# Output projection in 15 products a block: the last two heads' rows moved into spare rows by small DMAs

## The chip, the core and the metric

The kernel runs on one core of a Trainium2 chip. TensorE (PE in the profile, PEld for its weight loads), VectorE (DVE), ScalarE (ACT) and GpSimd (POOL) each work through their own list of instructions in order; SyncE (SP) does nothing but issue transfers. A transfer is issued by an instruction on SP's or ACT's list and carried out by 16 DMA engines. The metric is the time of one execution on the device, in microseconds (us), as the median of several runs.

## The reference

x has 2048 tokens of 640 features. Both branches read the normalised x; the result is x plus their product.

```python
def _A_ref(x, wqkv, w_phi, wo):                  # 32 heads of 20
    q, k, v = ...                                # x @ wqkv, per head
    pq = jnp.einsum("bhsd,hdf->bhsf", q, w_phi)
    pk = jnp.einsum("bhsd,hdf->bhsf", k, w_phi)
    phi_q = jnp.concatenate([_softmax(pq), _softmax(-pq)], axis=-1)   # 40 a head
    phi_k = jnp.concatenate([_softmax(pk), _softmax(-pk)], axis=-1)
    kv = jnp.einsum("bhsf,bhsd->bhfd", phi_k, v)
    z = jnp.einsum("bhsf->bhf", phi_k)
    num = jnp.einsum("bhqf,bhfd->bhqd", phi_q, kv)
    den = jnp.einsum("bhqf,bhf->bhq", phi_q, z)[..., None] + 1e-6
    return heads_joined(num / den) @ wo

xn = _layernorm(x)
s = _A_ref(xn, A_wqkv, A_w_phi, A_wo)
g = _silu(gelu(xn @ w1 + b1) @ w2 + b2)
return x + s * g
```

## The kernel before

The work is laid out by hand in the order in which PE runs it. First come keys, values and queries (up to about 238 us of the profile), with the state kv summed in PSUM and the exponentials of the queries stored in e_dram. Then follow twelve units of the MLP (`for unit in range(units)`, 238 to 555 us): in each, `part` makes the up products and `down` the down products (L998), whose sums VectorE adds to y (L1007). Beside the units the queries are normalised, one tile of 128 tokens after another: `q_load` (L1041), `q_norm` with a multiplication on GpSimd, sums on VectorE, a scaling on GpSimd, a transpose in blocks on VectorE (L1064), and four stores (L1069) into phi_t, which holds the query features with the tokens along the free axis. phi_t has one DRAM tensor for each of the four chunks of 512 tokens; chunk c holds tiles 4c to 4c+3. Tile 7, the last one, is done only after the units, by the generator `late_q`, one step of which runs after each block of the output projection (two steps after each of the first two).

The last stage, from 555 us on, is the subject. It takes the chunks in the order 2, 3, 0, 1 (ORDER). The loop at L1343 runs over the chunks, and within it over five blocks d of 128 output columns; blocks are numbered here 0 to 19 in the order of time.

- `load_phi` (L1091, L1093) loads a chunk's query features, 1280 rows: five tiles phT of 240 rows, three heads to each 60 rows of output, and a sixth with the last 80 rows (heads 30 and 31).
- `num` makes the state products: two for each of the five tiles (L1103, weights bdk), which give 64 rows of output each, of which 60 are heads and 4 are zeros; and two for the sixth (L1110, weights bdl), in which the two heads' 40 rows stand three times. ACT copies a PSUM bank rounded to fp32r (L1106, L1112), VectorE subtracts the copy from the bank (L1107, L1113), so that oT holds a high and a low part.
- `finish` is one block: 16 products (L1156), three for each of the five tiles (high by high, high by low, low by high) and one for the last 40 rows, whose three forms stand side by side in 120 rows. Its weight wol is made once by `make_wol` on VectorE (L1080, L1081). VectorE multiplies the sum by the gate (L1158), GpSimd adds x (L1159), SP stores (L1163). The last block runs in two halves of 256 columns.
- `first_num` makes the first chunk's state products within the last down products (`down` asks it for a step ahead of each of its five sums). For the others, `num` stands after the fourth block (d == 3) of the chunk before.
- `load_res` loads x (L1130) and, for the first two chunks, the gate (L1134), four blocks ahead; `gate` computes it on ACT for the other two (L1142).

All engines keep the written order here (`manual_schedule`). PSUM has eight banks (`bankB`), handed on as soon as what reads them is done.

Of the kernel before, what the change touches and what calls it, by code (L numbers as in the profile page):

```python
# [8 lines left out]
F32 = mybir.dt.float32  # L9
# [6 lines left out]
P = 128  # L16
# [30 lines left out]
def hedgehog_gated_mlp_kernel(ctx: ExitStack, tc: tile.TileContext, x, xt_in, wqk, bd, wv, wo, w1, b1, w2, b2, out_t):  # L47
# [72 lines left out]
    for h in range(3):  # L120
# [4 lines left out]
    lowsel = const.tile([P, 1], F32, name="lowsel")  # L125
    nc.gpsimd.memset(lowsel[:], -1.0)
    nc.gpsimd.affine_select(out=lowsel[:], in_=lowsel[:], pattern=[[0, 1]],
                            compare_op=OP.is_ge, fill=0.0, base=-80, channel_multiplier=1)
    midsel = const.tile([P, 1], F32, name="midsel")
    nc.gpsimd.memset(midsel[:], -1.0)  # L130
    nc.gpsimd.affine_select(out=midsel[:], in_=midsel[:], pattern=[[0, 1]],
                            compare_op=OP.is_ge, fill=0.0, base=-40, channel_multiplier=1)
    nc.gpsimd.affine_select(out=midsel[:], in_=midsel[:], pattern=[[0, 1]],
                            compare_op=OP.is_ge, fill=0.0, base=79, channel_multiplier=-1)
    const.tile([P, 8], F32, name="align")
    bdk = const.tile([P, 10, 64], F32, name="bdk")
    bdl = const.tile([P, 120], F32, name="bdl")
# [781 lines left out]
    def kv_state(kvr):  # L919
        nc.gpsimd.memset(bdk[:, :, 60:], 0.0)  # L920
        ps = bankB()
# [14 lines left out]
        for r in range(3):  # L936
            nc.vector.tensor_tensor(bdl[:80, 40 * r:40 * r + 40].rearrange("p (h d) -> p h d", d=20),
                                    ps[:80, None, 352:372].to_broadcast([80, 2, 20]),
                                    mask[:80, :2, None].to_broadcast([80, 2, 20]), op=OP.mult)
# [131 lines left out]
    def wol_raw():  # L1071
        raw = row([P, D], F32, "raw")
        for r in range(3):
            nc.sync.dma_start(raw[40 * r:40 * r + 40, :], wo[640:680, :])
        return raw

    def make_wol(raw):
        wol_h = row([P, D], F32R, "wolh")
        wol = row([P, D], F32R, "wol")
        nc.vector.tensor_copy(wol_h[:120, :], raw[:120, :])  # L1080
        nc.vector.scalar_tensor_tensor(wol[:120, :], wol_h[:120, :].bitcast(F32), midsel[:120, :], raw[:120, :],  # L1081
                                       op0=OP.mult, op1=OP.add)
        return wol


    def load_phi(c, js, home=None):
        out = {}
        for j in js:
            ph = slab(F32, "phT", (P, 2, CW)) if home is None else home.tile([P, 2, CW], F32, tag="L", name="phT")
            if j < 5:  # L1090
                nc.sync.dma_start(ph[:120], phi_t[c][240 * j:240 * j + 240, :].rearrange("(e p) t -> p e t", p=120))  # L1091
            else:
                nc.sync.dma_start(ph[:80, 0], phi_t[c][1200:, :])  # L1093
            out[j] = ph
        return out

    def num(phi, oT, js):
        for j in js:
            ph = phi.pop(j)
            po = bankB()  # L1100
            if j < 5:
                for e in range(2):
                    nc.tensor.matmul(po[64 * e:64 * e + 64, :], bdk[:120, 2 * j + e, :], ph[:120, e, :],  # L1103
                                     start=True, stop=True)
                o2 = oT[0][j]
                nc.scalar.activation(o2[:, 0], po[:], AF.Copy)  # L1106
                nc.vector.tensor_tensor(o2[:, 1], po[:], o2[:, 0].bitcast(F32), op=OP.subtract)  # L1107
            else:
                for a, b in ((0, 64), (64, 120)):
                    nc.tensor.matmul(po[a:b, :], bdl[:80, a:b], ph[:80, 0], start=True, stop=True)  # L1110
# [301 lines left out]
```

## Time and profile before

| | us |
|---|---|
| median of 3 runs (650.46 to 650.9) | 650.58 |
| span of the profiled execution | 649.0 |
| PE busy in it | 643.7 (99%) |
| last stage: start of the output projection to PE's end | 555.35 to 645.12 |
| output projection, all L1156 products, share of the chain that ended last | 11% |
| state products, L1103, share of the chain | 2% |
| transfers issued by SP, share of the 16 DMA engines, 520 to 650 us | 85.0% |

The profile has one row for an instruction or a group: start, busy time, engine, line, operation, output and inputs, and in brackets what ended the idle time before it. The chain of waits goes back from the last instruction, at each step to what released it. A product of full-precision fp32 (L1103, L1110) stands in it as two records. Rows of SPq and ACTq are issues of transfers; their duration is that of the issue, and the time to landing is a column of its own in the DMA and tile views.

### The profile page before, as it was taken

The page shows a single profiled execution, that of the slowest core. Times are in us where ns is not written, and L with a number is a line of the kernel's source. Part 1 is how long each engine was busy: PE and PEld are TensorE (multiplying, and loading weights), DVE is VectorE, ACT ScalarE, POOL GpSimd, SP SyncE. Part 2 cuts the span into 40 slices and gives each one's busy share as a digit, 9 for nine tenths or more (in the row PEclk, how much of TensorE's full clock was granted, in tenths as well). Part 3 has the DMA queues.
Part 4 walks back from the last instruction along what each step waited for, and adds up shares of the span by engine and source line. Part 5 has one row for each costly group of instructions (what it writes and reads, how often), then busy time and mean ns, then how long its engine had stood idle before and what let it go on. Part 6 is the DMA issues. An engine that isn't in the chain of part 4 may idle for free.

```text
span 649.0 us, 11412 instructions
## 1 busy us (share of the span) xinstructions
PE 643.7 (99%) x4379; PEld 559.1 (86%) x4379; DVE 485.1 (75%) x736; ACT 238.1 (37%) x345; POOL 408.9 (63%) x375
## 2 busy tenths in 40 slices
PE   9999999999999999999999999999999999999997
PEld 9999999999999998888888888888888886766866
DVE  5887976789867787587988877768889899853132
ACT  3622423425243447244243346641231524032130
POOL 2876477897987756857878865355463966342321
PEclk9999999999999999999999999999999999999999
DMA  9477286494312477365986998794969499999952
GB/s 346 113 238 228 57 303 197 107 309 147 123 42 74 152 263 262 103 217 170 317 236 236 254 409 285 144 350 163 183 238 243 67 267 198 304 242 248 291 207 81
DMA packets 167119, 136.53 MB, mean 210 GB/s; under 512 B 89890, under 2 KB 131106, under 8 KB 166682
## 3 DMA queue, kind: packets, MB, share of 16 engines
q1 hardware_dynamic: 164330, 124.22, 65.9%
q10 hardware_dynamic: 2736, 11.60, 4.8%
q8 instruction: 34, 0.56, 0.4%
q14 instruction: 19, 0.16, 0.1%
HBM read 87.41 MB, written 48.38 MB: 209 GB/s over the span
## 4 chain that ended last, share of the span: by engine, by line
PE 96%; DMA 1%; DVE 1%; SPq 0%; issue 0%; DVEq 0%
PE pB L998 24%; PE pA L411 23%; PE pB L969 23%; PE pB L1156 11%; PE pA L724 6%; PE pB L1103 2%; PE pA L174 2%; PE kv L491 2%; PE qV L724 1%; DMA folds<-in_wqk_dram 1%; PE qY L724 1%; DVE y L1007 1%; PE pB L1110 1%; DMA phi_t<-eq 0%; PE pA L397 0%; DVE wolh L1080 0%
## 5 line engine op out<-in xcount | busy, mean ns | idle before, releaser
L998 PE MATMUL pB<-hs,w2s 128*128 128x512 f32 x720 | 165.7, 389 | 0.0
L998 PEld LDWEIGHTS pB<-hs,w2s 128*128 128x128 f32 x720 | 135.0, 188 | 28.8 <-DVE y L1007 0.8
L969 PE MATMUL pB<-xp,w1s 128*128 128x512 f32 x324 | 81.3, 389 | 0.0
L969 PE MATMUL pB<-xd,w1s 128*128 128x512 f32 x324 | 79.3, 389 | 0.0
L452 POOL TENSOR_TENSOR eq<-eq,rc 128x1280 f32<-128x1280 f32 x16 | 37.9, 2368 | 55.3 <-DVE rc L1060 38.1
L1156 PE MATMUL pB<-oT,wo 128*128 128x512 f32 (+1 forms) x315 | 72.3, 381 | 0.0
L969 PEld LDWEIGHTS pB<-xd,w1s 128*128 128x128 f32 x324 | 60.8, 188 | 12.6
L969 PEld LDWEIGHTS pB<-xp,w1s 128*128 128x128 f32 x324 | 60.8, 188 | 12.6
L1156 PEld LDWEIGHTS pB<-oT,wo 128*128 128x128 f32 x315 | 57.2, 188 | 13.8 <-PE pB L1103 2.5
L1007 DVE TENSOR_TENSOR y<-pB,y 128x512 f32<-128x512 f32 x100 | 63.1, 676 | 1.4 <-PE pB L998 1.4
L974 ACT ACTIVATE pB<-pB,b1t 128x512 f32<-128x512 f32 x48 | 31.8, 662 | 78.8 <-DVE pB L1237 28.9
L411 PE MATMUL pA<-wk,xp 128*128 128x320 f32 x384 | 59.6, 310 | 0.0
L439 ACT ACTIVATE e<-e 128x1280 f32<-128x1280 f32 x32 | 40.6, 1272 | 50.0 <-POOL e L430 50.0
L411 PEld LDWEIGHTS pA<-wk,xp 128*128 128x128 f32 x384 | 56.9, 188 | 0.1
L430 POOL TENSOR_TENSOR e<-nr,e 128x640 f32<-128x640 f32 x32 | 46.0, 1437 | 16.4 <-DVE nr L429 16.3
L452 POOL TENSOR_TENSOR e<-e,rc 128x1280 f32<-128x1280 f32 x16 | 37.8, 2369 | 20.2 <-DVE rc L479 20.2
L1047 POOL TENSOR_TENSOR ez<-eq,zrep 128x1280 f32<-128x1280 f32 x16 | 47.3, 2959 | 2.0 <-DMA eq<-e_dram 2.0
L519 POOL TENSOR_TENSOR w1s<-raw,w1s 128x640 fp32r<-128x640 f32 (+1 forms) x18 | 26.2, 1458 | 27.6 <-ACT w1s L518 27.6
L411 PE MATMUL pA<-wv,xp 128*128 128x320 f32 x240 | 37.0, 310 | 0.0
L1159 POOL TENSOR_TENSOR xres<-gt,xres 128x256 f32<-128x256 f32 x20 | 14.3, 735 | 35.3 <-DVE gt L1158 24.9
L149 POOL TENSOR_TENSOR w2s<-raw,w2s 128x640 fp32r<-128x640 f32 x23 | 36.1, 1592 | 0.2 <-ACT w2s L147 0.2
L411 PEld LDWEIGHTS pA<-wv,xp 128*128 128x128 f32 x240 | 35.5, 188 | 0.1
(190 smaller groups left out, 1140.4 us busy)
## 6 DMA issues: line engine op xcount, KB each, us to landing
raw<-in_w_dram SPq DMA_DIRECT2D x42, 320.0 KB, 6.7
e_dram<-e ACTq DMA_DIRECT2D x16, 640.0 KB, 3.9
eq<-e_dram SPq DMA_DIRECT2D x16, 640.0 KB
phi_t<-eq SPq DMA_DIRECT2D x64, 160.0 KB, 4.3
phT<-phi_t SPq DMA_DIRECT2D x20, 480.0 KB, 10.1
xt<-in_x_dram SPq DMA_DIRECT2D x16, 320.0 KB, 6.1
xres<-in_xt_dram SPq DMA_DIRECT2D x20, 256.0 KB, 9.1
out_dram<-xres SPq DMA_DIRECT2D x18, 256.0 KB, 5.1
```

The costliest lines, as they stand in the source:

```text
L149: eng.tensor_tensor(sl[:, 1, :], raw, sl[:, 0, :].bitcast(F32), op=OP.subtract)
L411: nc.tensor.matmul(ps[:, hf, :HALF], stat_x(q, o, k, a), ws[k][:, b, hf * HALF:(hf + 1) * HALF], start=n == 0, stop=n == 3 * KC - 1)
L430: rest = lambda: nc.gpsimd.tensor_tensor(e5[:, :, :, 1, :], nr[:, :, :, None].to_broadcast([P, 2, 16, DH]), e5[:, :, :, 0, :], op=OP.subtract)
L439: nc.scalar.activation(ef, ef, AF.Exp)
L452: nc.gpsimd.tensor_tensor(e3, e3, rc[:, :, None].to_broadcast([P, 64, DH]), op=OP.mult)
L724: nc.tensor.matmul(bank[ch], q_x(blk, a, q), p_weight(base, f, w, k)[:, b], start=ch not in seen and n == 0, stop=n == len(mms) - 1, skip_ ...
L969: nc.tensor.matmul(bank[ch][:], tl[:, a, off + wo_:off + wo_ + P], mov(blk, b), start=new and n == 0, stop=n == len(mms) - 1, skip_group_c ...
L974: nc.scalar.activation(ps, ps, AF.Gelu_apprx_tanh, bias=b1t[:, f:f + 1])
L998: nc.tensor.matmul(ps[:], ws[i][:, b, d * P:(d + 1) * P], hs[o][i][:, a, :], start=i == n == 0, stop=(i, n) == (GF - 1, 2), skip_group_che ...
L1007: nc.vector.tensor_tensor(y, ps[:], y, op=OP.add)
L1047: nc.gpsimd.tensor_tensor(zv, ef, zf, op=OP.mult)
L1156: nc.tensor.matmul(ps[:, mv], w, o[:, mv], start=n == 0, stop=n == 15, skip_group_check=True)
```

## The change

The two heads that had a 16th product of their own are put into the rows that stood at zero: each of the ten 64-row groups has four spare rows, and 10 x 4 = 40. The weight wo gets rows 600 to 639 in these places (in the host's layout), and a block has 15 products. The 40 rows of the output come from `num_rest`: one pair of state products for two chunks at once, the first chunk's in rows 0 to 63 and the second's in rows 64 to 127 of one bank, split into high and low part oR as before. `put_rest` then moves four rows of oR into each half of each oT tile by a DMA on ACT's queue, ten a chunk of 4 rows x 4 KB, each once the tile's own split is written.

The order changes with it. `load_rest` loads the last 80 rows for two chunks: for chunks 2 and 3 on SP's queue in the last unit, for chunks 0 and 1 on ACT's queue after block 5. The pair of `num_rest` for chunks 0 and 1 stands on PE after block 7, before that chunk's other state products. `num` stands after the third block of the chunk before (d == 2, not 3), and in `first_num` one step earlier. `late_q` takes two steps after each of the first three blocks, not only after the first two, so the stores of tile 7 come after block 3 and not after block 4. wol, its loads, and the masks lowsel and midsel are gone.

```diff
 def kv_state(kvr):
     nc.gpsimd.memset(bdk[:, :, 60:], 0.0)
+    nc.gpsimd.memset(bdl[:, 40:], 0.0)
...
-        for r in range(3):
-            nc.vector.tensor_tensor(bdl[:80, 40 * r:40 * r + 40].rearrange("p (h d) -> p h d", d=20),
+        nc.vector.tensor_tensor(bdl[:80, :40].rearrange("p (h d) -> p h d", d=20),
...
+    def load_rest(cs, eng):
+        ph = slab(F32, "phR", (P, 2, CW))
+        for c in cs:
+            eng.dma_start(ph[:80, c % 2], phi_t[c][1200:, :])
+        return ph
+
+    def num_rest(ph):
+        po = bankB()
+        for e in range(2):
+            nc.tensor.matmul(po[64 * e:64 * e + 64, :], bdl[:80, :], ph[:80, e, :], start=True, stop=True)
+        o2 = slab(F32R, "oR", (P, 2, CW))
+        split_o(po, o2)
+        return o2
+
+    def split_o(po, o2):
+        nc.scalar.activation(o2[:, 0], po[:], AF.Copy)
+        nc.vector.tensor_tensor(o2[:, 1], po[:], o2[:, 0].bitcast(F32), op=OP.subtract)
+
+    def num(c, phi, oT, oR):
+        for j in range(KC):
+            ph = phi.pop(j)
+            po = bankB()
+            for e in range(2):
+                nc.tensor.matmul(po[64 * e:64 * e + 64, :], bdk[:120, 2 * j + e, :], ph[:120, e, :],
+                                 start=True, stop=True)
+            split_o(po, oT[j])
+            if j:
+                put_rest(c, j - 1, oT, oR)
+        put_rest(c, KC - 1, oT, oR)
+
+    def put_rest(c, j, oT, oR):
+        for e in range(2):
+            r = 64 * (c % 2) + 4 * (2 * j + e)
+            nc.scalar.dma_start(oT[j][64 * e + 60:64 * e + 64].bitcast(F32), oR[r:r + 4].bitcast(F32))
...
-        steps = [(wo_s[j][:, b, d * P:(d + 1) * P], oT[0][j][:, a, :]) for j in range(5) for a, b in PASSES]
-        steps.append((wols[0][:120, d * P:(d + 1) * P], oT[1][:120, 1, :]))
+        steps = [(wo_s[j][:, b, d * P:(d + 1) * P], oT[j][:, a, :]) for j in range(KC) for a, b in PASSES]
...
-            phi = load_phi(ORDER[0], range(6))
+            phi = load_phi(ORDER[0], range(KC))
+            phr = load_rest(ORDER[:2], nc.sync)
...
-        if not more:
-            wolr = wol_raw()
...
     def first_num():
-        wols.append(make_wol(wolr))
-        yield
-        yield
-        yield
-        num(phi, oT, range(6))
+        oR.append(num_rest(phr))
+        yield
+        yield
+        num(ORDER[0], phi, oT, oR[-1])
         yield
...
-            if ci == 0 and d < 2:
+            if ci == 0 and d < 3:
                 next(lq, None)
...
-            if ci + 1 < NCH and d == 3:
-                num(phin, oTn, range(6))
-            if ci + 2 < NCH and d == 3:
+            if ci == 1 and d == 0:
+                phr = load_rest(ORDER[2:], nc.scalar)
+            if ci + 1 < NCH and d == 2:
+                if ci == 1:
+                    oR.append(num_rest(phr))
+                num(ORDER[ci + 1], phin, oTn, oR[-1])
+            if ci + 2 < NCH and d == 2:
                 phin = {**phi, **load_phi(ORDER[ci + 2], JB)}
...
-    wo = np.zeros((680, D), a["wo"].dtype)
+    wo = np.zeros((D, D), a["wo"].dtype)
     for k in range(10):
         wo[64 * k:64 * k + 60] = a["wo"][60 * k:60 * k + 60]
-    wo[640:] = a["wo"][600:]
+        wo[64 * k + 60:64 * k + 64] = a["wo"][600 + 4 * k:604 + 4 * k]
```

More of the change, by code (lines that the diff above doesn't have):

```diff
@@ L1100, in num @@
             po = bankB()
[L1101 to L1110, printed above, removed]
-                o2 = oT[1]
-                nc.scalar.activation(o2[:120, 0], po[:120], AF.Copy)
-                nc.vector.scalar_tensor_tensor(o2[:120, 1], o2[:120, 0].bitcast(F32), lowsel[:120, :],
-                                               po[:120], op0=OP.mult, op1=OP.add)
```

48 lines of the change are left out of this document (11 added, 37 removed).

## Prediction

> **What bounds the kernel now.** I read the page first, then the chain of work that ended last, then the DMA queue of SP and the waits of the last 100 us, because the change touches only what starts at about 540 us.
>
> ```profile
> span 649.0 us, 11412 instructions
> PE 643.7 (99%) x4379; PEld 559.1 (86%) x4379; DVE 485.1 (75%) x736; ACT 238.1 (37%) x345; POOL 408.9 (63%) x375
> ```
>
> PE is busy for 99% of the span, so work taken from PE shortens the kernel, unless PE then has to wait. The end of the chain shows what that work is:
>
> ```profile
> 552.40 2.95 PE pB L998 x12
> 555.35 14.59 PE pB L1156 x64
> 569.93 4.44 PE pB L1103 x20
> 574.38 0.86 PE pB L1110 x4
> 575.24 18.47 PE pB L1156 x80
> ...
> 622.78 22.33 PE pB L1156 x112
> 645.12 0.02 issue
> ```
>
> L998 are the last down products, L1156 is the output projection (16 products a block), L1103 and L1110 are the state products of a chunk. One product costs 18.47/80 = 0.231 us, one block 3.69 us. PE goes from one row to the next without a gap.
>
> The second thing that the stage hangs on is the transfers. All of them are issued by SP, and they fill the DMA engines (the DMA view of 562 to 600 us: queue, packets, MB, share of the 16 engines):
>
> ```profile
> q1 hardware_dynamic: 14696, 9.37, 99.3%
> ```
>
> SP's queue in order of time (start, duration of the issue, line), and what SP waited for (total, times, longest):
>
> ```profile
> 546.88 1.82 SPq L1091 DMA_DIRECT2D phT<-phi_t  x3
> 548.75 0.43 SPq L1041 DMA_DIRECT2D eq<-e_dram  x1
> 549.28 0.59 SPq L1130 DMA_DIRECT2D xres<-in_xt_dram  x1
> 549.97 0.37 SPq L1134 DMA_DIRECT2D gt<-g_dram  x1
> 550.43 0.51 SPq L1130 DMA_DIRECT2D xres<-in_xt_dram  x1
> 551.00 0.73 SPq L1134 DMA_DIRECT2D gt<-g_dram  x1
> 551.96 0.33 SPq L1130 DMA_DIRECT2D xres<-in_xt_dram  x1
> 554.10 0.32 SPq L1134 DMA_DIRECT2D gt<-g_dram  x1
> 556.16 0.33 SPq L1130 DMA_DIRECT2D xres<-in_xt_dram  x1
> ```
> ```profile
> SPq L1134 <- DMA phT<-phi_t: 1.7, 1, 1.7
> ```
> ```profile
> SPq L946 <- DMA e_dram<-e: 5.0, 1, 5.0
> ```
>
> Eight issues follow each other closely. The ninth, tenth and eleventh (551.96, 554.10, 556.16) come 2.1 us apart, and the waits name the landing of phT as what released the gt load (554.10), which has no data in common with phT. So an issue waits until the eighth issue before it has landed. The third fence (waits of 225 to 260 us) shows that ACT's issues are in the same count: L946 writes z_dram from kvr, and waited 5.0 us for e_dram<-e, which ACT had issued.
>
> **What the change removes.** Nineteen blocks lose a product of 0.231 us. The last block runs in two halves: 22.33 us are five blocks of 3.69 and 32 half products, 0.12 each, of which two go. Together 19 x 0.231 + 0.24 = 4.6 us. L1110 has two products a chunk at 0.86 us; eight become four, 1.7 us less. PE loses 6.3 us. The two operations that prepare wol (L1080, L1081) leave VectorE. PE's timeline and VectorE's, where the first chunk's state products began:
>
> ```profile
> 546.42 4.51 PE L1103 MATMUL pB<-phT,bdk 120*64 120x512 f32 x20
> ```
> ```profile
> 546.73 1.27 DVE L1007 TENSOR_TENSOR y<-pB,y 128x512 f32<-128x512 f32 x2
> ```
>
> The chain runs through PE without a gap from 552.40 on, so VectorE's lost work buys nothing after that. The state products of the first chunk now come twelve down products earlier, and need five PSUM banks while three are held by half-finished sums; the last two become free with the y additions that end at 548.0 us. PE would be there at 542.3 + 0.86 (spare state products) + 1.4 (six down products) + 1.8 (the first two state products) = 546.4, where 542.3 is 546.42, the start of L1103, less 18 down products of 0.23 (the L998 row of the chain has 2.95/12 = 0.25 with a wait in it, the block's product 0.231). I charge 0.6 us; if VectorE is later, up to 1.5. The setup of lowsel and midsel on GpSimd at the start, the memset and the one bdl operation instead of three in the middle: no PE instruction waits there, zero. Row and queue space: SP loses the three loads of wol and four loads of the last rows and gains two; zero by themselves, counted below.
>
> **What it adds, first: the small transfers.** put_rest issues ten a chunk ("puts" below), 16 KB each, on ACT's queue between the copies of the state products, each behind the VectorE subtraction of its tile.
>
> ```profile
> L1106 ACT ACTIVATE oT<-pB x20: 597/597/603, 547.5 to 622.0; 128x512 fp32r<-128x512 f32 x20
> ```
> ```profile
> L756 ACTq DMA_DIRECT2D e_dram<-e x13: 326/327/333, 95.6 to 238.6; - x13
> ```
> ```profile
> DMA to landing us min/median/max: 2.3/5.6/9.1
> ```
>
> (The last line is the tile view of xres.) A tile costs ACT 0.60 + 2 x 0.33 = 1.3 us, 6.3 us a chunk; PE needs 4.44 us for the same tiles and then has two blocks of 3.46 before it reads the result, so issue and a landing of 2.3 would be hidden. The places among the eight are not: a put of the first chunk waits for the eighth issue before it, and these are the loads of 549 to 556 us and the next, the later of which land about 9 us after their issue. The last puts go out at 560 to 562 and land at 562 to 564, where block 0 asks for the last tile at 556.0 + 12 x 0.231 = 558.8. That is a stall of about 5 us (bounds 0 and 8), and behind a waiting put on ACT stand the next copies, behind these the VectorE subtractions.
>
> **Second: the state products of the spare rows for the last two chunks.** They stand on PE after block 7 and read chunk 1's rows of phi_t, so they need the four stores of token tile 7. Before, nothing read these stores until the state products after block 13. SP around them, and the tile view of eq:
>
> ```profile
> 585.11 0.42 SPq L1093 DMA_DIRECT2D phT<-phi_t  x1
> 586.68 0.36 SPq L1130 DMA_DIRECT2D xres<-in_xt_dram  x1
> 588.77 0.34 SPq L1134 DMA_DIRECT2D gt<-g_dram  x1
> 589.21 0.38 SPq L1163 DMA_DIRECT2D out_dram<-xres  x1
> 589.69 6.59 SPq L1069 DMA_DIRECT2D phi_t<-eq  x4
> ```
> ```profile
> L1069 SPq DMA_DIRECT2D phi_t<-eq x16: 318/846/4533, 538.5 to 595.5; - x16
> ...
> DMA to landing us min/median/max: 4.6/5.6/6.7
> ```
>
> The last store is issued at 595.5 and lands at 595.5 + 4.6 = 600.1 or later. The change takes the four issues in front (585.11 to 589.21) out of its way: the L1093 load goes, and block 8's loads and block 4's output now come behind the stores. That makes it at most 4.6 us earlier. Against it, the second chunk's ten puts now stand just in front of them and take places among the eight; that gives back between nothing and all. I take the middle, 2.3 us: landed at 597.8. Then ACT, which has waited at its DMA instruction with nothing else to do, issues (0.3 us) the load of 160 KB.
>
> ```profile
> e_dram<-e ACTq DMA_DIRECT2D x16, 640.0 KB, 3.9
> ...
> phT<-phi_t SPq DMA_DIRECT2D x20, 480.0 KB, 10.1
> ```
>
> These page rows (KB, us to landing) are the neighbours: 10.1 for loads of the same kind behind SP's backlog, 3.9 for what ACT issued on its own queue, 2.3 the quickest xres. I take 3.9, the row of the same queue, and keep 2.3 and 10.1 for the range: the rows are there at 602.0. [...]
>
> **The sum.** The blocks began at 555.35 (chain), now 556.0 with the 0.6 us. PE would reach the spare state products, with no stall on the way, at 556.0 + 3 x 3.46 + 4.44 + 5 x 3.46 = 588.1; with 5 us at block 0, at 593. Both are before 602.0, so the stall at block 0 is inside the wait for the rows and not added. After 602.0: 0.86 + 2 x 4.44 + 11 x 3.46 + 3.6 (the halved block) = 51.4 us, PE ends at 653.4, and from PE's end at 645.1 to the end of the span it was 3.9 us: span 657.3. The profiled execution before had 649.0 for a median of 650.6, 1.6 more: **659.0 us**, 8.4 slower. So 6.3 us are saved, and PE waits 14.
>
> **Rivals.**
> *Transfers in time (faster).* If tile 7's stores and the load are done by 588.1, all 6.3 us but the 0.6 remain: 650.6 - 5.7 = 644.9. For it: the stores come a block earlier. Against: the load would have to land 14 us earlier than reckoned, with the engines 99.3% taken and only three transfers and a 160 KB load out of the way. It decides where the rows land: by 594 the result is no change, earlier it is a gain.
> *ACT and SP hold each other.* If the second chunk's puts wait for the long phT loads, and SP's stores then wait for the puts, the stores come later than before, not sooner: with another 5 us on the 4.6 bound, landed at 605, the end is at about 666. For it: every put stands eight behind a load that takes 9 us. Against: a put gives its place back in 2.3.
> *The clock drops in the wait.* Window, busy time of PE, PEld, DVE, ACT, POOL, granted clock, DMA share, GB/s:
>
> ```profile
> 645.00:647.00 2.00, 0.10 (x1) 0.00 (x0) 0.85 (x2) 0.00 (x0) 0.00 (x0) 1.00 0.23 81
> 647.00:649.00 2.00, 0.00 (x0) 0.00 (x0) 0.00 (x0) 0.00 (x0) 0.00 (x0) 0.66 0.14 50
> ```
>
> After PE's end the granted clock holds for 2 us and then falls; if it falls to half, a mean of 0.66 puts that 2.5 us after the last product. A wait of 8 to 14 us would be enough. If the half rate lasts as long again once PE resumes, 2.5 us of work take 1.25 longer: 660.3. [...] No row here shows PE resuming after a wait that long.
> *It does not do what it says.* The products do go from PE; nothing speaks for this.
>
> **How the numbers follow.** About 0.2% (1.3 us) is what a measurement of this kernel can tell from no change. Chances: the forecast as it stands 0.53 (655 to 663, the bounds of the stores and of the load), with the clock's drop on top 0.12, ACT and SP holding each other 0.2 (up to 672), transfers in time 0.11, rows landing between 592 and 595, no change, 0.04. The range from 650 to 668 leaves out the fast case and the end of the slow one.
>
> **What would show it.** Right: L1156's product at 0.231 us in 15s; a PE wait of 8 us or more in front of the second pair of spare state products, released by ACT's phi_t load, which itself was released by phi_t<-eq; a smaller wait at block 0 for the puts; SP's issue of tile 7's stores between 585 and 590. Wrong: no such wait, because the stores land by 588; or a wait that starts earlier and is that of the puts in every chunk.

## The result and the profile after

| | us |
|---|---|
| before, median of 4 runs (650.46 to 650.90) | 650.74 |
| after, median of 4 runs (681.67 to 686.51) | 684.93 |
| ratio, 95% interval | 1.0522 (1.0492 to 1.0552) |
| span of the profiled execution after (its time 686.36) | 684.4 |

The change makes the kernel 34.2 us slower. In code lines of the changed kernel, L1143 is the product of the output projection, L1093 and L1079 are the state products and the spare ones, L1103 the puts, L1085 and L1086 the copy and the subtraction, L1060 the stores of phi_t, L1150 the output store.

The timeline of PE in the last stage (start, busy time, in brackets the idle time ahead and what ended it):

```profile
545.00 1.44 PE L1079 MATMUL pB<-phR,bdl 80*64 80x512 f32 x4 [1.89 <-DMA phR<-phi_t]
...
569.85 1.62 PE L1143 MATMUL pB<-oT,wo 128*128 128x512 f32 x3 [10.17 <-DMA oT<-oR]
574.80 12.61 PE L1143 MATMUL pB<-oT,wo 128*128 128x512 f32 x42 [3.34 <-DMA oT<-oR]
...
602.25 4.18 PE L1143 MATMUL pB<-oT,wo 128*128 128x512 f32 x9 [3.37 <-DMA oT<-oR]
609.63 10.87 PE L1143 MATMUL pB<-oT,wo 128*128 128x512 f32 x36 [3.19 <-DMA oT<-oR]
620.42 1.55 PE L1079 MATMUL pB<-phR,bdl 80*64 80x512 f32 x3
...
656.41 24.29 PE L1143 MATMUL pB<-oT,wo 128*128 128x512 f32 x120
```

Block 0 starts at 569.85, not at 555.35. Every chunk but the last waits for puts (oT<-oR), 24.4 us in all by the source view of L1103, whose first row also has a put's time on ACT's list (min, median, max in ns):

```profile
L1103 ACTq DMA_DIRECT2D oT<-oR x40: 584/584/1191, 563.3 to 660.4; - x40
...
  PE pB L1143: 24.4, 6
```

Where that begins and how it spreads is in three timelines, of ACT, GpSimd and SP:

```profile
551.49 0.60 ACT L1085 ACTIVATE oT<-pB 128x512 fp32r<-128x512 f32 x1 [0.26 <-PE pB L1093]
563.27 1.91 ACTq L1103 DMA_DIRECT2D oT<-oR  x2
565.22 0.60 ACT L1085 ACTIVATE oT<-pB 128x512 fp32r<-128x512 f32 x1 [13.13 <-DMA oT<-oR]
...
572.04 4.30 ACTq L1103 DMA_DIRECT2D oT<-oR  x4
```
```profile
580.91 1.44 POOL L1146 TENSOR_TENSOR xres<-gt,xres 128x256 f32<-128x256 f32 x2 [30.98 <-DVE gt L1145]
```
```profile
569.42 0.34 SPq L1122 DMA_DIRECT2D gt<-g_dram  x1
582.38 0.34 SPq L1150 DMA_DIRECT2D out_dram<-xres  x1
582.81 3.39 SPq L1060 DMA_DIRECT2D phi_t<-eq  x4
...
608.79 4.10 SPq L1060 DMA_DIRECT2D phi_t<-eq  x4
```

ACT has two copies done by 552.1 and then stands at its first put until 563.27: the eighth issue before it is the load of eq, whose place it needs; both signal the same semaphore, and by the trace's semaphore events that load landed at 563.19. The three copies behind that put come at 565 to 571, the last four of the ten puts leave from 572.04 on, the products wait for both, and block 0's sum leaves GpSimd at 580.91 + 1.44 = 582.35. On SP's list block 0's output stands ahead of the stores and of the next chunk's loads, so SP issues nothing from 569.8 to 582.38. (The view of SP's waits books these 12.8 us under oT<-oR; the issue follows GpSimd's add by 0.03 us, and that is what it waited for.) The later transfers are late with it: token tile 7's stores, at 589.69 before, come at 608.79, the last line above (those at 582.81 are token tile 6's).

The fourth thing to see is the clock. Window, busy PE, PEld, DVE, ACT, POOL, granted clock, DMA share, GB/s, first of the changed kernel, then one window of the kernel before:

```profile
555.00:570.00 15.00, 4.83 (x22) 3.73 (x21) 1.38 (x2) 1.19 (x2) 0.00 (x0) 0.79 1.03 295
570.00:588.00 18.00, 14.66 (x49) 10.60 (x51) 9.77 (x14) 0.60 (x1) 5.75 (x5) 0.70 0.51 108
...
602.00:620.00 18.00, 14.55 (x44) 11.18 (x45) 3.53 (x9) 0.07 (x1) 5.63 (x8) 0.64 0.97 226
```
```profile
570.00:588.00 18.00, 18.00 (x80) 12.08 (x80) 8.12 (x15) 5.60 (x8) 7.09 (x9) 1.00 0.98 260
```

After these waits the products run slower for a while: 42 of them took 12.61 us, where 0.231 each makes 9.7, and the granted clock is 0.50 from 563.7 to 580.6 and again from 601.2 to 614.8. And in the window in which SP stands still the DMA share is 0.51, where it was 0.98 before.

The wait that the forecast put its weight on, at the second pair of spare state products, hardly shows: PE gets there at 620.42 with no idle time, and one weight load waits 0.7 us for the rows of chunk 1, which landed at 621.29.

### The profile page after: what moved, and what is told of

The parts are those of the page before. It is cut to its first block, busy times and chain, and to the rows that moved or that the text cites. A ratio compares the mean times of both kernels' runs of the same rounds, so it can differ in the third digit from the quotient of the medians.

```text
span 684.4 us, 11407 instructions
## 1 busy us (share of the span) xinstructions
PE 650.9 (95%) x4350; PEld 560.3 (82%) x4350; DVE 483.3 (71%) x730; ACT 236.7 (35%) x343; POOL 407.7 (60%) x371
## 4 chain that ended last, share of the span: by engine, by line
PE 78%; DMA 13%; DVE 3%; POOL 2%; issue 2%; ACT 1%; SPq 1%; ACTq 0%; POOLq 0%
PE pA L402 22%; PE pB L960 17%; PE pB L989 17%; PE pB L1143 8%; PE pA L715 6%; DMA phT<-phi_t 2%; DMA oT<-oR 2%; DMA phR<-phi_t 2%; DMA xres<-in_xt_dram 2%; PE pB L1093 2%; PE pA L165 2%; PE kv L482 2%; PE qV L715 1%; DMA gt<-g_dram 1%; DMA w_dram<-w1s 1%
## 5 line engine op out<-in xcount | busy, mean ns | idle before, releaser
L1143 PE MATMUL pB<-oT,wo 128*128 128x512 f32 (+1 forms) x315 | 80.2, 417 | 25.9 <-DMA oT<-oR 24.4
L1143 PEld LDWEIGHTS pB<-oT,wo 128*128 128x128 f32 x315 | 62.6, 209 | 44.9 <-issue 13.8
L1086 DVE TENSOR_TENSOR oT<-pB,oT 128x512 fp32r<-128x512 f32 x20 | 13.7, 689 | 37.5 <-ACT oT L1085 37.4
L1085 ACT ACTIVATE oT<-pB 128x512 fp32r<-128x512 f32 x20 | 11.9, 597 | 70.6 <-DMA oT<-oR 27.1
```

Of the source, the lines that this page charges most:

```text
L1143: nc.tensor.matmul(ps[:, mv], w, o[:, mv], start=n == 0, stop=n == 3 * KC - 1, skip_group_check=True)
```

## The experiments

**First, the puts, the rows behind token tile 7, ACT's order, the saving.** Theory: the puts and the shared count of eight. Rivals: the forecast's own step; copies standing behind puts; the landing of a small transfer. The ratios in this part are to runs of the kernel before that were taken beside each kernel.

```diff
-            if j:
-                put_rest(c, j - 1, oT, oR)
-        put_rest(c, KC - 1, oT, oR)
```

> The changed kernel without its forty puts; everything else stays, the spare state products and the load of their rows too (the last two heads' rows never reach the output projection, so their part of the output is left out). Theory now (the puts hold places in the count of eight that ACT's and SP's queues share, and the two queues wait for each other through it): all of the loss over the forecast's own step goes, first block without its 10 us wait, and every later wait of L1143 for oT<-oR is gone: 645 to 648 us if the rows of the second spare pair are there in time. My forecast's step (PE waits at the second pair of spare state products for the stores of token tile 7 and the 160 KB load behind them): PE gets there at about 588 and waits 8 to 14 us: 655 to 660. Both may hold at once; then it is 655 to 660 with a wait of PE released by phR<-phi_t, and the 25 us above that are the puts'.

It took 670.0 us (ratio 1.0311, 1.029 to 1.0333). Without puts the forecast's wait is there, in full (two lines of PE's timeline; then token tile 7's stores on SP's list, for which the rows of chunk 1 wait):

```profile
592.46 1.04 PE L1079 MATMUL pB<-phR,bdl 80*64 80x512 f32 x2 [0.69 <-DMA phR<-phi_t]
610.31 1.11 PE L1079 MATMUL pB<-phR,bdl 80*64 80x512 f32 x1 [16.81 <-DMA phR<-phi_t]
```
```profile
591.03 8.09 SPq L1060 DMA_DIRECT2D phi_t<-eq  x4
```

So the two causes don't add: in the changed kernel PE is so late from the puts that chunk 1's rows are there. It is worse than either expectation, so something else is lost too.

The puts on another queue, with a count of its own:

```diff
-            nc.scalar.dma_start(oT[j][64 * e + 60:...
+            nc.gpsimd.dma_start(oT[j][64 * e + 60:...
```

> The changed kernel with the same forty puts issued from GpSimd's queue, whose transfers are counted on eight places of their own; nothing is left out. Theory now (shared places): ACT's copies and SP's transfers stand as in the kernel without puts, so the time is that kernel's plus what the landing of the last puts costs block 0 and a little at each chunk: at most 5 us more than it. Rival, the landing itself (5 to 7 us each for so small a transfer, whatever counts it): waits of L1143 for oT<-oR stay at 10 us at block 0 and 3 us at each later place, 670 us or more. Rival, the queue in which a put stands blocks what is behind it: GpSimd's adds (L1146) come late and with them the output stores, 655 to 670.

673.7 us (1.0364, 1.0345 to 1.0383): 11 us better than on ACT's queue, 3.7 above the kernel without puts. The first two rows are GpSimd's timeline, the third is the source view of the puts, the fourth PE's timeline:

```profile
553.73 4.31 POOL L1103 DMA_DIRECT2D oT<-oR  x8 [3.92 <-DVE oT L1086]
562.46 1.10 POOL L1103 DMA_DIRECT2D oT<-oR  x2 [4.43 <-DMA oT<-oR]
```
```profile
DMA to landing us min/median/max: 2.1/7.1/11.0
```
```profile
596.65 4.59 PE L1143 MATMUL pB<-oT,wo 128*128 128x512 f32 x12 [7.78 <-DMA oT<-oR]
```

The first put leaves at 553.73, not at 563.27, so the places are a cause. Eight puts leave in a row and the ninth waits for a put to land: GpSimd has eight places of its own. But a put lands here 7.1 us after its issue at the median, not 2.3, so the landing is one too: block 0 still waits 3.6 us in three pieces, the second chunk 10.8.

```diff
-            if j:
-                put_rest(c, j - 1, oT, oR)
-        put_rest(c, KC - 1, oT, oR)
+        for j in range(KC):
+            put_rest(c, j, oT, oR)
```

> The changed kernel with the ten puts of a chunk issued on ACT behind all five of its copies, not between them. Rival (the loss comes from copies of ACT standing behind puts in ACT's queue): the copies and the VectorE subtractions are done as soon as the state products are, and of the 34 us most goes: 655 or less. Theory now (places of the shared count, SP's queue held): the puts still wait for the eighth issue before them and SP's next issue for a put's place, so the block 0 wait stays at 8 us or more and the transfers stay late: 670 to 685.

687.3 us (1.0573, 1.0548 to 1.0597), with a wait of 16.2 us ahead of block 0. The rival of ACT's order falls.

```diff
-        steps.append((wols[0][:120, d * P:(d + 1) * P], oT[1][:120, 1, :]))
```

> The kernel before with the 16th product of each output block left out (the last two heads' low part doesn't reach the output), all loads, state products and splits as they were. It gives the price of the one product on PE by itself: 4.6 us of PE (19 x 0.231 + 0.24) if blocks of the output projection are bound by PE, 646.1 us; 650.5 if something else sets their end.

645.96 us (0.9932, 0.9915 to 0.9949). The saving is real where nothing else changes: 4.3 us against the runs of before beside it (650.26), where the prediction's sum has 4.6 for these products.

**Second, the rows of the second pair chunk by chunk.** The spare products of chunk 0 and of chunk 1 are made each with its own chunk, their rows loaded on SP ahead of that chunk's phT.

```diff
...
+            phrs[ci + 2] = load_rest(ORDER[ci + 2:ci + 3], nc.sync)
...
-                if ci == 1:
-                    oR.append(num_rest(phr))
+                if ci:
+                    oR.append(num_rest(phrs.pop(ci + 1), (ORDER[ci + 1] % 2,)))
```

> The changed kernel without its puts (the last two heads' rows don't reach the output projection, so their part of the output is left out), and with the second pair of spare state products taken apart: chunk 0's rows loaded on SP's queue in front of chunk 0's phT loads and multiplied with chunk 0's state products, chunk 1's likewise with chunk 1's. The kernel without puts alone took 670.0, with a 16.8 us wait of PE for phR at 593. Theory (that wait is my forecast's one, the rows behind the stores of token tile 7): the wait goes and 17 to 20 us with it, 648 to 652; what stays above 645 is the 1.7 us at the first pair and 1 to 2 us at the second chunk. Rival (the wait only moves on to the loads of the last chunk's phT, which stand behind the same stores): 655 to 668.

> The changed kernel with its puts as they are and the second pair of spare state products taken apart as in the kernel above; nothing left out. Theory (in the changed kernel the stall of the puts covers the wait for chunk 1's rows, so the two are not added): only the little that was still to be seen of that wait goes, 680 to 685. If the two add up: 17 us less, 668 or below.

> As the kernel above, with the puts on GpSimd's queue, with its own eight places; nothing left out. The kernel with GpSimd's puts alone took 673.7: 3.6 us of waits at block 0, 10.8 in the second chunk, 1.1 for phR, 2.2 in the third. Theory (the price that is left is the landing of a put under load, 8 to 11 us against 6.9 us of cover by two blocks): these waits stay as they are and it comes to 665 to 672. Rival (the second chunk's puts were late because of the phR load and its wait): below 660.

Without puts 656.9 us (1.0086, 1.0061 to 1.0111): 13.1 of the 670.0 go, so the forecast's wait is shown, at nearly its forecast size. With the puts on ACT 687.5 (1.0563, 1.0548 to 1.0578): nothing gained, the one wait did cover the other. With the puts on GpSimd 664.3 (1.021, 1.0174 to 1.0247). On top of 656.9, then, the puts cost 30.5 us on ACT's queue and 7.4 on GpSimd's. But 656.9 is still 11 us more than 645.96, with 6.8 us of waits for phT and phR loads.

```diff
...
-                nc.tensor.matmul(po[64 * e:64 * e + 64, :], bdk[:120, 2 * j + e, :], ph[:120, e, :],
-                                 start=True, stop=True)
-            split_o(po, oT[j])
+                f = 180 * j + 60 * e
+                nc.tensor.matmul(po[:120, :], bdkf[:120, f:f + 120], ph[:120, e, :], start=e == 0, stop=e == 1)
+            split_o(po, oT[j], 0, 120)
...
+            nc.gpsimd.dma_start(oT[j][120:].bitcast(F32), oR[r:r + 8].bitcast(F32))
```

> A version meant to keep the saving; nothing left out. The spare rows are the last eight of each tile (both state products of a tile accumulate into rows 0 to 119, as many products as before), so a chunk has five puts of 32 KB, not ten of 16; the copies write rows 0 to 119 only, so that a put waits for the spare state products alone; these stand two to three blocks ahead of the chunk's other state products (one for the last chunk), which are back behind the fourth block; puts on GpSimd's queue, the spare rows loaded chunk by chunk on SP's. Theory (the 6.3 us of PE are there, and what ate them was waits that can all be covered): no wait of the output projection for oT<-oR above 1 us, 644 to 648. Rival (the transfers added to full DMA rings cost by themselves, wherever they stand): 652 or more, with waits for phT or phR.

661.1 us (1.0155, 1.0141 to 1.0169). No wait at all is left in the last stage, as the theory had it, but "as many products as before" was my error:

```profile
572.55 8.75 PE L1097 MATMUL pB<-phT,bdk 120*120 120x512 f32 x20
```

The same 20 records took 4.51 us where each pair wrote 64 columns of its own. What follows such a group starts 8.19 us after its start here and 4.44 there, so 4 x 3.75 = 15 us are lost; without them I estimate 646. The slabs of this kernel start at a multiple of 1024 bytes (8192), as those of the kernel before do (7168); those of the changed kernel lie 32 bytes below one, and the fifth part measures what that costs.

**Third, the layout of the change with early puts; the state products back in place.** The copies and subtractions are made on rows 0 to 59 and 64 to 123, so that the puts wait for the spare products alone. The edit shown is that of the first version, with the puts on GpSimd's queue. The second kernel has no puts and only the move of the state products to `d == 3`; the third is the first with its puts on ACT's queue.

```diff
-            split_o(po, oT[j])
+            split_o(po, oT[j], 0, 60)
+            split_o(po, oT[j], 64, 124)
...
+            if ci + 1 < NCH and d == (0, 1, 2)[ci]:
+                if ci:
+                    oR.append(num_rest(phrs.pop(ci + 1), (ORDER[ci + 1] % 2,)))
+                put_rest(ORDER[ci + 1], oTn, oR[-1])
-            if ci + 1 < NCH and d == 2:
+            if ci + 1 < NCH and d == 3:
                 num(ORDER[ci + 1], phin, oTn, oR[-1])
```

> A second version meant to keep the saving; nothing left out. The version with eight spare rows at a tile's end had no wait of PE for phT, phR or oT in the output projection, but its state products took 8.75 us a chunk, not 4.51, because two products into the same 120 columns no longer ran side by side. Here the tile is laid out as in the changed kernel again (two products of 64 columns, ten puts of four rows), and each copy and subtraction is made twice, on rows 0 to 59 and 64 to 123, so that the puts wait for the spare products alone; the rest as in that version. Theory: its 661.1 less 4 x 4.2 us of state products, 643 to 646, without a wait above 1 us. Rival (the twice as many copies on ACT and VectorE, or ten puts in place of five, make a wait of their own): 650 or more.

> The kernel without puts and with the spare products chunk by chunk (656.9; the last two heads' part of the output is left out), with each chunk's state products back behind the block where they stood before the change, one block later. In that kernel PE still waited 6.4 us for phT loads in the three later chunks. Theory (the move of the state products a block forward, which my forecast put at nothing, brings them in front of their loads): these waits go, 645 to 650, the rest being the 1.5 us at the first pair. Rival (the loads are late because the phR loads stand in front of them, wherever the products stand): 654 or more.

> The second version with its early puts on ACT's queue, in the shared count of eight, in place of GpSimd's; nothing left out. Theory (a put in the shared count holds SP's transfers up and is held up by them, however early it is asked for): waits of PE for oT<-oR or for phT come back, 655 or more. Rival (only the lateness of the puts did the harm; issued two blocks ahead they cost nothing): within 2 us of the version on GpSimd's queue.

Early puts on GpSimd: 666.3 us (1.0239, 1.0221 to 1.0258), the rival: block 0 still waited 3.6 us for puts, the second chunk 4.4 and four times 0.4 for copies. The same on ACT: 707.3 (1.0871, 1.0855 to 1.0886), the worst of all:

```profile
580.27 5.22 PE L989 MATMUL pB<-hs,w2s 128*128 128x512 f32 x12 [22.36 <-DVE oT L1086]
```

Here ACT stands at its puts while the copies that would free PE's banks wait behind them. Asking earlier does not help the puts on ACT's queue; whether the shared count or ACT's order does the harm, this run does not separate. The move of the state products alone, without puts: 656.1 (1.0089, 1.0058 to 1.0119). The rival; the waits only moved, to 5.8 us at two phT loads that had come behind tile 7's stores.

```diff
+            for a in (0, 64):
+                nc.scalar.activation(oT[j][a:a + 60, 0], po[a:a + 60], AF.Copy)
+            for a in (0, 64):
+                nc.vector.tensor_tensor(oT[j][a:a + 60, 1], ...
...
+            phr = load_rest(ORDER[:2], nc.sync)
             phi = load_phi(ORDER[0], range(KC))
-            phr = load_rest(ORDER[:2], nc.sync)
...
```

> The second version (early puts on GpSimd's queue, 666.3) mended in three places that its trace showed; nothing left out. The two copies of a tile stand together on ACT and the two subtractions behind them on VectorE (there each half waited for the other engine, 2.07 us a tile); the first pair's rows are loaded in front of chunk 2's phT and multiplied in front of the last down products, so that the first chunk's puts leave earlier (there 3.6 us of waits at block 0); the last two phT loads of chunk 0 are asked for a block earlier, in front of the stores of token tile 7. Theory (all waits are covered): 643 to 648. Rival (the second chunk's copies still come late, 4.4 us there, because the subtractions stand in VectorE's order behind a transposition of the last token tile that waits for GpSimd, which is busy issuing puts): 651 to 658.

662.0 us (1.0169, 1.0152 to 1.0186), not the theory: 4.4 us at block 0 for puts that left from 549.6 on, and the second chunk's wait as the rival had it.

**Fourth, loads and puts earlier still.**

```diff
+            if ci + 2 < NCH and d == 2:
+                phi.update(load_phi(ORDER[ci + 2], JB))
...
```

> The kernel without puts, spare products chunk by chunk and state products back behind the fourth block of a chunk (656.1; the last two heads' part of the output is left out), with the last two phT loads of chunk 0 asked for one block earlier, so that SP issues them in front of the stores of token tile 7. There PE waited 5.8 us for them at 602. Theory (of what the kernel without puts still loses, most is the order of the loads on SP's queue): the wait goes, 646 to 650, about the 646.0 of the kernel before with 15 products plus the 1.2 us at the first pair. Rival (the loss is the fuller DMA rings, the order only moves it): 653 or more.

```diff
+        if not more:
+            oT = new_oT(late)
+            oR = [num_rest(phr)]
+            put_rest(ORDER[0], oT, oR[0])
+            wo_s = [split_w(r[:], "wo", "pool", late) for j, r in enumerate(wo_r)]
         dn = down(g, w2g, hs, 0)
...
+    oTn = new_oT(slabs)
+    put_rest(ORDER[1], oTn, oR[0])
     for ci, c in enumerate(ORDER):
```

> The mended second version (662.0) with its puts moved further ahead; nothing left out. The first pair's rows are loaded in front of the wo weights and multiplied a unit part earlier, and the first chunk's puts stand on GpSimd's queue in front of the wo splits, so that they are issued at about 539, not 549.6; the second chunk's puts follow in front of block 0, about 17 us earlier, where they no longer hold up token tile 7's steps on GpSimd. Theory (every put that has its landing of 10 us ahead of its reader costs nothing): no wait for oT<-oR, 644 to 649, faster than both kernels. Rival (the puts hold up what stands behind them on GpSimd, the wo splits or block 0's adds, or wait for buffers): 652 or more, with a wait of PE for wo or for a PSUM bank at block 0.

The first took 656.9 us (1.0096, 1.0069 to 1.0123): the waits for phT went and came back as 5.2 us of waits behind gt loads. The second took 662.5 (1.0191, 1.0172 to 1.021). In it the puts cost block 0 nothing any more (issued at 541.6, 14 us ahead), and there too a load was late instead:

```profile
555.90 13.76 PE L1145 MATMUL pB<-oT,wo 128*128 128x512 f32 x60
569.59 2.80 PE L1093 MATMUL pB<-phT,bdk 120*64 120x512 f32 x12
576.88 3.98 PE L1093 MATMUL pB<-phT,bdk 120*64 120x512 f32 x8 [4.50 <-DMA phT<-phi_t]
```

Whatever I moved, some load was late, in kernels whose loads were hardly more than before. What they had in common stood in lines of the change that the prediction passes over; it counts the setup of lowsel and midsel at zero, because no PE instruction waits there, and does not ask where the buffers behind them then lie:

```diff
-    lowsel = const.tile([P, 1], F32, name="lowsel")
-    midsel = const.tile([P, 1], F32, name="midsel")
-    const.tile([P, 8], F32, name="align")
+    const.tile([P, 10], F32, name="align")
-    bdl = const.tile([P, 120], F32, name="bdl")
+    bdl = const.tile([P, 64], F32, name="bdl")
+    const.tile([P, 56], F32, name="align2")
```

In columns of 4 bytes the sum is the same, 770. But in the two programs as built each mask of 4 bytes takes up 32 (lowsel starts at byte 2336 of a partition, midsel at 2368), and the padding takes 32 before (2400 to 2432) and 64 after (2336 to 2400): every later buffer starts 32 bytes lower, the first of the slabs at 7136 and not at 7168.

**Fifth, the 32 bytes.** The first pair of lines below is the edit of the changed kernel and of the two others that have the shift undone; the last line is that of the kernel before, which is shifted by it.

```diff
-    const.tile([P, 10], F32, name="align")
+    const.tile([P, 24], F32, name="align")
...
-    const.tile([P, 8], F32, name="align")
```

> The changed kernel with 32 bytes more of padding in front of its buffers in the on-chip memory; nothing else. The change takes out two one-column tiles and resizes the padding, and all later buffers start 32 bytes lower: the first of them at byte 7136 of a partition, not 7168 (7 x 1024). In every kernel that starts at 7136 the stores of phi_t land 1.14 to 1.20 us apart on the mean, in the three that start at a multiple of 1024 (the kernel before, it with 15 products, the version with eight spare rows) 0.99 to 1.01. Theory (shifted buffers slow the transfers, on top of what the puts do): stores 1.0 us apart again, and the time falls by what the fuller rings cost, 8 to 15 us: 670 to 677. Rival (the spacing of the stores is a mark of the other changes and not of the address): no change, 682 to 687.

> The kernel before with its padding tile of 32 bytes left out, so that all later buffers start at 7136; nothing else. Theory (the address slows the transfers by itself): stores of phi_t 1.15 to 1.2 us apart, waits of PE for phT or for gt in the output projection, 655 to 662. Rival (the address does nothing): 650.7.

> The kernel without puts, with the spare products chunk by chunk and the phT loads asked for earlier (656.9; the last two heads' part of the output is left out), with the buffers back at a multiple of 1024. Theory (the shift is what it still loses): no wait of the output projection for gt, 645 to 647, as the kernel before with 15 products. Rival: 655 to 658.

> The version with all puts issued more than 10 us ahead on GpSimd's queue (662.5), with the buffers back at a multiple of 1024; nothing left out. There block 0 had no wait for oT<-oR any more, but PE waited 4.5 us for phT in the second chunk's state products and 4.1 us for VectorE behind a late gt load in the third chunk. Theory (both are the slower transfers): these waits go, 645 to 649, faster than both kernels. Rival (forty puts fill the rings whatever the address): 655 or more.

The changed kernel with the 32 bytes back: 674.85 us (1.0371, 1.0356 to 1.0385), 10.1 less. The kernel before without them: 657.1 (1.0091, 1.0065 to 1.0117), 6.4 more. The page's row of SP's queue in the kernel before, and in it shifted (packets, MB, share of 16 engines):

```profile
q1 hardware_dynamic: 164330, 124.22, 65.9%
```
```profile
q1 hardware_dynamic: 164330, 124.22, 67.3%
```

The same packets and bytes take 0.673 x 655.7 = 441.3 us of the engines, not 0.659 x 649.0 = 427.7: 3.2% more. By the packets of the two traces it falls on small ones: those of 128 bytes, the stores' runs of 32 fp32 values, go from 13.37 to 13.99 ns on the mean, those of 512 bytes from 27.41 to 29.35, those of 2,560 not up at all (115.35 and 114.49). The landings of the phi_t stores are 1.15 us apart on the mean, not 1.00, and the issue of one on SP's list takes 1005 ns at the median, not 783 (source views of the store's line):

```profile
L1069 SPq DMA_DIRECT2D phi_t<-eq x64: 318/783/9264, 305.4 to 595.5; - x64
```
```profile
L1068 SPq DMA_DIRECT2D phi_t<-eq x64: 318/1005/9317, 305.3 to 603.6; - x64
```

Without puts, aligned: 645.76 us (0.9931, 0.9911 to 0.9951), 11.2 less than shifted and the same as the kernel before with 15 products. So for the version without puts nothing is left over: with the address right, no spare row moved and the spare products chunk by chunk, the change would be worth its 5 us.

What the puts do in the changed kernel with the address right, on PE's timeline:

```profile
563.20 1.62 PE L1143 MATMUL pB<-oT,wo 128*128 128x512 f32 x3 [7.71 <-DMA oT<-oR]
568.47 11.86 PE L1143 MATMUL pB<-oT,wo 128*128 128x512 f32 x42 [3.66 <-DMA oT<-oR]
...
593.82 2.38 PE L1143 MATMUL pB<-oT,wo 128*128 128x512 f32 x9 [2.02 <-DMA oT<-oR]
601.24 11.12 PE L1143 MATMUL pB<-oT,wo 128*128 128x512 f32 x36 [5.04 <-DMA oT<-oR]
612.29 1.08 PE L1079 MATMUL pB<-phR,bdl 80*64 80x512 f32 x4
```

Block 0 waits 11.4 us, the second chunk 7.1, and then the spare products nothing. Of the 10.1 us between the two versions, 4.2 are there before the first wait for a put: PE's last products ahead of block 0 end at 559.69 shifted and at 555.50 aligned, and the first pair of spare products waits 1.89 us for its rows shifted and not at all aligned.

The version with early puts, aligned: 654.3 us (1.0047, 1.0033 to 1.0061), 8.2 less than shifted and still 3.6 above the kernel before. No wait for phT or gt or oT above 0.4 us is left in the last stage; one wait ahead of it decides, PE's, VectorE's and GpSimd's timelines:

```profile
554.02 1.98 PE L1093 MATMUL pB<-phT,bdk 120*64 120x512 f32 x4 [5.68 <-DVE y L998]
```
```profile
544.69 8.67 DVE L1051 TENSOR_TENSOR rc<-rc,den 128x64 f32<-128x64 f32 x1
```
```profile
545.77 7.50 POOL L140 TENSOR_TENSOR wo<-raw,wo 128x640 fp32r<-128x640 f32 x5
```

A VectorE multiplication that takes 0.22 us at the median ends only when GpSimd's five do (553.36 and 553.27), and GpSimd begins these at 545.77, not at 539.04 as in the kernel before, because ten puts stand ahead of them (5.32 us from 540.43). In the kernel before the same two end at 546.80 and 546.72, in the changed kernel at 547.43 and 547.35, where the multiplication takes 1.13 and 1.11 us. That GpSimd holds VectorE is my reading of these ends; no run varies it. So no version here beats the kernel before with all that it computes.

## Why the prediction was wrong

Slower was right. The size was not: 684.9 lies far above 668, the end of the range. Worked back over the medians, the 34.2 us are: -5.0 for the work saved (650.74 to 645.76), +29.1 for the puts and what they set off (645.76 to 674.85), +10.1 for the address (674.85 to 684.93). The middle term is between two kernels that differ in the puts and also in when the second pair's rows are loaded; with the address right no run separates these. In shifted kernels with the rows chunk by chunk the puts alone cost 30.5 (656.91 to 687.45).

- *6.3 us saved on PE.* Nearly right: 5.0 in the kernel without puts, in which one of the two pairs is taken apart again. A pair side by side does cost about one, 1.08 us where each chunk took 1.03.
- *0.6 us for PSUM banks.* Not seen; with the address right PE goes from the state products of chunk 2 to block 0 with no wait but the puts'. The two figures that the prediction takes it from, 548.0 and 546.4, differ by 1.6 and not by 0.6.
- *A stall of about 5 us at block 0 (bounds 0 and 8).* The step that failed first. Measured 13.5, and 11.4 with the address right. The forecast had the last of the ten puts leave by 560 to 562; the first left at 563.27 and the last four from 572.04 on. I had rightly found that a put waits for the eighth issue before it, then let each place come back in 2.3 us. The load of eq kept its place for 9.6 us (553.55 to 563.19), and the first chunk's puts landed 2.2 to 7.4 us after their issue on ACT's queue by the semaphore events, 2.1 to 11.0 with a median of 7.1 over all puts on GpSimd's. The 2.3 us is no load's landing either: that view of xres mixes loads with output stores, and the quickest row is an output store of 632.44, late in the stage; the only load in it took 9.1. An issue on ACT took 0.584 us, not 0.33.
- *"The stall at block 0 is inside the wait for the rows and not added."* The logic held, with the roles changed: the stall covered the wait. It failed in counting the puts once. The next two chunks wait as well (24.4 us in the three), which stands last among the prediction's own signs of being wrong, and block 0's lateness goes through its output store on SP's list into every later transfer.
- *PE waits 14 us at the second spare pair.* Right as a mechanism and nearly in size (16.8 us, worth 13.1), in a kernel that has no puts. The size is in part luck: that kernel is shifted, and both ends of the wait are late, PE there at 592.46 and not 588.1, the rows used at 610.31 and not 602.0. In the changed kernel one weight load waits 0.7 there.
- *The rival "ACT and SP hold each other".* This is what happened, given 0.2 and an end at 672. My reason against it, that a put gives its place back in 2.3 us, was the same wrong row. The path back from ACT to SP is not the count alone, though, as I had it in the first expectations: it goes through block 0's output.
- *The rival "the clock drops in the wait".* True as well, and several times over, with a granted clock of 0.64 to 0.79 in windows with waits.
- *What no step had:* the 10.1 us of the address. The prediction took every duration of before to hold after, counted the setup of lowsel and midsel at zero, and never priced the lines that change the padding.

What stays open: why the address costs 10.1 us in the changed kernel, 11.2 in the one without puts, 8.2 in the one with early puts and 6.4 in the kernel before, so that the puts don't explain the difference; which boundary counts, as only buffers from a multiple of 1024 on and 32 bytes below were run; and whether puts on ACT would cost as much if the address were right and the rows came chunk by chunk.

## What to carry to other kernels

A transfer on a path that PE reads soon is priced by its landing at that time of the program, under that load (here 2.1 to 11.0 us for a put of 16 KB), and by the eighth issue before it in the order of both queues (here the first put left at 563.27, when the load of eq had landed at 563.19), and then followed to what stands behind its reader on every list. The two waits at different places of one path did not add here; the earlier one hid the later (0.7 us of it was left), which came out in full (16.8) once the first was cured. An edit that only removes small tiles can move the address of every buffer behind them, here by 32 bytes, which cost 10.1 us: compare addresses before comparing anything else.

## What the runs showed of the hardware

- *32 bytes.* Kernels whose slabs start at 7136 had mean distances between landings of phi_t stores of 1.14 to 1.20 us (in the changed kernel 1.17 without two gaps of over 2 us, 1.23 with them), the six that start at a multiple of 1024 had 0.99 to 1.02. The times of the shifted kernel before scatter more, 653.69 to 659.0 and not 650.56 to 651.25, but the aligned kernel without puts ran from 644.77 to 650.64, so that scatter is not the address alone. In the shifted kernel before, packets of 128 and 512 bytes took longer (13.37 to 13.99 ns, 27.41 to 29.35), those of 2,560 did not (115.35 and 114.49). Why the small ones do, and which boundary counts, no run tells.
- *Landing under load.* The same put of 16 KB landed 2.1 to 11.0 us after its issue, on GpSimd's queue.
- *Two products of 64 columns ran side by side.* 4.51 us for 20 records, those of the two products of a pair beginning 0.007 us apart (546.422 and 546.429 in the kernel before), one such pair of records 0.43 us after the other; 8.75 us when each pair wrote into the same 120 columns.
- *VectorE beside GpSimd.* 8.67 us for an instruction of 0.22 (median of 16 in the kernel before). By its record the multiplication began at 544.69, 1.08 us before the first of the five GpSimd instructions, and ended at 553.36, 0.09 us after the last of them (553.27); the kernel before and the changed one show the same ends 0.08 us apart. What ties the two, no run shows.
